# Layer 2 by Strassen's seven products, with statistics on ScalarE and listed orders

## The chip, the cores and the metric

One Trainium2 chip; the kernel runs on one of its cores. The core's engines each work through an instruction queue of their own: TensorE (PE in the profile; PEld are its weight loads), VectorE (DVE), ScalarE (ACT), GpSimd (POOL) and SyncE (SP, which here only issues DMAs). They wait for one another through semaphores. A matmul here multiplies a stationary block of 128 x 128, loaded beforehand, with up to 512 moving columns, and writes into PSUM; the kernel uses 8 PSUM banks of 512 f32 columns on 128 partitions.

The metric is the device time of one execution in microseconds (us). The kernel before takes 298.35 us, the median of three runs (297.99 to 298.51).

## The reference

Two blocks follow each other. The first is a cross attention between 512 tokens and 32 state rows, in 8 batches of 8 heads of 64. The second adds the real part of a two-dimensional Fourier transform to its input, normalises each row and sends it through two dense layers.

```
# block 1, per batch and head: x (512 x 64), state (32 x 64)
a  = softmax(scale * x @ state.T);  xread = a  @ state
a2 = softmax(scale * state @ x.T);  sread = a2 @ x
X  = concat([xread, sread])          # 544 rows; heads side by side: 512 columns
# block 2, per batch: X (544 x 512)
u  = X + real(fft(fft(X, axis=rows), axis=columns))
un = (u - mean(u)) / sqrt(var(u) + 1e-6)          # per row
out = u + relu(un @ w1) @ w2                      # w1 512 x 2048, w2 2048 x 512
```

The output is 8 x 544 x 512 in f32. The matmuls work on bf16.

## The kernel before

The 544 rows of a batch are worked as four row tiles of 128 and 32 left over; the left-over rows of four batches make one tile of 128, the "L" tiles, which come in stages 3 and 7. The kernel runs in stages, one a batch. In stage `b` these stand beside one another: layer 2 of batch `b-1`, layer 1 of batch `b`, the second half of the attention and the Fourier transform of batch `b+1`, the first half of the attention (scores) of batch `b+2`, and loads of x for batch `b+3`.

What the change and the prediction's steps touch, by name and line:

- `layer1(key)`, L908: 16 steps of four 512-column matmuls into `ph` (L920), each followed by a relu on ScalarE into `hT` (L922), which holds the 2048 hidden values of 512 rows, hidden index on the partitions, in bf16. In `hT[:, f, rows]`, `f` counts 16 blocks of 128 hidden values.
- `layer2(key)`, L941: for each row tile `i`, 16 matmuls of 512 columns into one bank `po` (L985), `hT`'s block stationary and `w2`'s rows moving; then `store` (L946) lets VectorE compute `ot = po * rstd + u` (L952) and issues the output DMAs. Rows that come out in reversed order go to `r_dram` first and from there to `out`. The last row tile of the last batch is split into 384 and 128 columns (L977).
- `transform(b)`, L689: the Fourier transform of a batch. `over_s` (`gp`, L774) and `over_d` (`yp`, L670 and L671) are its matmuls. `add` (L675, L682) adds the input rows to give `u`. `centre` (L825) takes the row's mean and variance with VectorE (`bn_stats` L337, `bn_aggr` L339), the reciprocal root on GpSimd (L343, L344), and writes `ub`, the centred rows in bf16, on VectorE (L833) or, for batches 1 and 2, on ScalarE (L831). `turn_u` (L835, the DMA L838) transposes `ub` into `unT` by a DMA. Only batch 0 uses `add_sums`, which takes the row sums in the same pass as the addition (L793), and `centre_sums`, which centres by `-512 u + sum` (L808 to L814) and leaves the factor -1/512 to layer 1's relu.
- `attend(b)`: `scores` (`esp`), `turn_scores` (`eTp`), `xread` (`xfp`, `xrp`, L447; evictions L456), `sread_by_head` (`srp`, L467; L474), and the folds of rows and columns that prepare the Fourier transform (`Sm`, `SS`, `XE`, `XO`, `XQ`, L516 to L536 on VectorE; `XT`, `XEl`, `XOl`, `XQl`, L501 to L513 on GpSimd).

The order is the order in which the Python code calls the engines: written out by hand up to stage 1, and from stage 2 on by `weave`, which sorts the steps of several lists by a position between 0 and 1 that is spread evenly over a range given for each list. All engines keep this order, each for its own instructions; nothing is moved by a scheduler.

PSUM: two banks for `psX`, three for `psQ` and three for `psF` (from which `ph` and `po` come). The pools hand out their buffers in turn. In SBUF the tags `xs`, `xT`, `E`, `ET` and `hT` have two buffers each, `ot` four and `ub` five.

Of the kernel before, what the change touches and what calls it, by code (L numbers as in the profile page):

```python
# [12 lines left out]
F32 = mybir.dt.float32  # L13
BF16 = mybir.dt.bfloat16
I32 = mybir.dt.int32
AF = mybir.ActivationFunctionType
ALU = mybir.AluOpType
PI = math.pi

@with_exitstack  # L30
def kernel(
# [8 lines left out]
    nc = tc.nc  # L40
# [16 lines left out]
    wk = ctx.enter_context(tc.tile_pool(name="wk", bufs=2))  # L57
    opening = ExitStack()
# [628 lines left out]
    flipped = (0, 1, 2)  # L687

    def transform(b):  # L689
# [8 lines left out]
        order = [(0, 1), (1, 0), (0, 0), (1, 1)] if b == B - 1 else [(0, 1), (0, 0), (1, 1), (1, 0)]  # L698
# [135 lines left out]

        def turn_u(k, r, copy=nc.vector.tensor_copy):  # L835
            col = order.index((k, r)) * 128
            if b >= u_by_dma:
                nc.sync.dma_start_transpose(out=unT[:, :, col:col + 128], in_=ub[k, r])  # L838
                return
            tp = qt("tp", BF16)  # L840
            for j in range(DC):
                nc.tensor.transpose(tp[:, 128 * j:128 * j + 128], ub[k, r][:, 128 * j:128 * j + 128], ident)
            copy(unT[:, :, col:col + 128], tp[:, 0:512].rearrange("p (a b) -> p a b", b=128))
# [20 lines left out]
        if b == 2:  # L864
# [7 lines left out]
            lambda: (over_d(0), add(0, 1), add(0, 0)),  # L872
            lambda: centre(0, 1),
            lambda: (centre(0, 0), over_d(1), add(1, 1), add(1, 0)),
            lambda: (turn_u(0, 1), centre(1, 1)),
            lambda: (turn_u(0, 0), centre(1, 0)),
            lambda: turn_u(1, 1),
            lambda: turn_u(1, 0),
# [29 lines left out]
    def layer1(key):  # L908
# [6 lines left out]
        def step(i):  # L915
            ph = psF.tile([128, 512], F32, name="ph", tag="c")
            for f in range(per * i, per * i + per):
                o = (f % per) * n
                for c in range(DC):
# [3 lines left out]
                                 scale=-1.0 / 512 if key == 0 else -1.0 if key in flipped else 1.0)  # L923

        def quarter_step(i, r):
            ph = psF.tile([128, 512], F32, name="ph", tag="c")
            for f in range(4 * i, 4 * i + 4):
                o = 128 * (f % 4)
                for c in range(DC):
# [3 lines left out]
                                 AF.Relu, scale=-1.0 / 512 if key == 0 else -1.0 if key in flipped else 1.0)  # L933
# [5 lines left out]
    later = []  # L939

    def layer2(key):  # L941
# [4 lines left out]
        def store(i, cols):  # L946
# [4 lines left out]
            ot = wk.tile([128, dm], F32, name="ot", tag="ot", bufs=4)  # L951
            nc.vector.scalar_tensor_tensor(ot[:, cols], in0=po_of[i][:, 0:cols.stop - cols.start], scalar=rstd,  # L952
                                           in1=u[:, cols], op0=ALU.mult, op1=ALU.add)
            queue = nc.scalar if key == B - 1 else nc.sync
            if isinstance(dst, bass.AP):
                nc.sync.dma_start(out=dst[:, cols], in_=ot[:, cols])
            elif isinstance(dst, int):
                nc.sync.dma_start(out=l_dram[dst].rearrange("b r n -> (b r) n"), in_=ot)
                for a in range(2):
                    nc.sync.dma_start(out=out[4 * dst:4 * dst + 4, 129 + 272 * a:144 + 272 * a, :].rearrange("b r n -> r b n"),  # L960
                                      in_=l_dram[dst, :, 16 * a:16 * a + 15, :].rearrange("b r n -> r b n"))
                    nc.sync.dma_start(out=out[4 * dst:4 * dst + 4, 272 * a, :].rearrange("b (c n) -> c b n", c=16),
                                      in_=l_dram[dst, :, 16 * a + 15, :].rearrange("b (c n) -> c b n", c=16))
            else:
                b, k, top = dst
                queue.dma_start(out=r_dram[b, k], in_=ot)
                later.append(lambda: queue.dma_start(
                    out=out[b, top:top - 128:-1, :].rearrange("r (c n) -> c r n", c=16),
                    in_=r_dram[b, k].rearrange("r (c n) -> c r n", c=16)))

        def step(i, q):
            if key == B - 1 and i == n - 1:
                cols = slice(0, 384) if q < 2 else slice(384, 512)
                if q % 2 == 0:
                    po_of[i] = psF.tile([128, dm], F32, name="po", tag="c")
                for f in range(8 * (q % 2), 8 * (q % 2) + 8):
                    nc.tensor.matmul(po_of[i][:, 0:cols.stop - cols.start], lhsT=h_of[key][:, f, i * 128:(i + 1) * 128], rhs=w2[:, f, cols],  # L977
                                     start=(f == 0), stop=(f == FC - 1))
                if q % 2:
                    store(i, cols)  # L980
                return
# [9 lines left out]


# [107 lines left out]
    warm(8)  # L1100
    opening.close()
    psX = ctx.enter_context(tc.tile_pool(name="psX", bufs=1, space=bass.MemoryType.PSUM))
    psQ = ctx.enter_context(tc.tile_pool(name="psQ", bufs=3, space=bass.MemoryType.PSUM))
    psF = ctx.enter_context(tc.tile_pool(name="psF", bufs=3, space=bass.MemoryType.PSUM))
# [116 lines left out]
    for b in range(1, B + 1):  # L1221
        reads_next = reads_after
        l2, l2_now = (layer2(b), [l2[7]] + l2[8:]) if b == 1 else (layer2(b) if b < B else [], l2)
# [3 lines left out]
        if b == 1:  # L1227
# [14 lines left out]
            for step in (spreads, M1[2], s2[0], s2[1], L1[0], M1[3], s2[2], s2[3], L1[1], lambda: cast_x(3), turned[3], L1[2],  # L1242
# [7 lines left out]
                step()  # L1250
            continue
# [6 lines left out]
        if b + 2 < B:  # L1258
            scores_next, reads_after = attend(b + 2)
            streams.append(([lambda: (cast_x(b + 2), turned[b + 2]())], 0.2, 0.2))  # L1260
            streams.append((scores_next, 0.5, 1))
        if b + 3 < B:
            streams.append(([lambda: load_x(b + 3)], 0.35, 0.35))
# [3 lines left out]
        weave(*streams)  # L1267

# [29 lines left out]
```

The softmax here doesn't subtract the row's maximum and nothing guards it: scores larger than these inputs give would overflow.

## Time and profile before

| what | us |
|---|---|
| median of three runs | 298.35 |
| span of the profiled execution, first to last instruction | 296.4 |
| 0 to 30: busy PE / DVE / ACT / POOL | 24.9 / 20.9 / 24.0 / 18.9 |
| 30 to 292.8: busy PE / DVE / ACT / POOL | 262.1 / 154.3 / 116.3 / 73.0 |
| 292.8 to 296.4, the last eviction and output write: PE / DVE | 0.2 / 0.35 |
| 139 to 171, one steady stage: busy PE / DVE / ACT / POOL | 32.0 / 19.2 / 13.5 / 7.9 |
| 267 to 293, the last batch's layer 2: busy PE / DVE / ACT / POOL | 26.0 / 4.4 / 4.8 / 0.0 |

The granted TensorE clock was 1.0 in every slice. In the profile a group of instructions stands as line, engine, operation, what it writes and reads, the shape, the count, then its busy time, the mean duration of one in ns, and the idle time of its engine just before, with what ended it. A timeline row has start, duration, engine, line, operation and count; rows of one kind that follow each other are merged. A matmul's duration includes the time in which the next one already runs.

### The profile page before, as it was taken

The page shows a single profiled execution, that of the slowest core. Times are in us where ns is not written, and L with a number is a line of the kernel's source. Part 1 is how long each engine was busy: PE and PEld are TensorE (multiplying, and loading weights), DVE is VectorE, ACT ScalarE, POOL GpSimd, SP SyncE. Part 2 cuts the span into 40 slices and gives each one's busy share as a digit, 9 for nine tenths or more (in the row PEclk, how much of TensorE's full clock was granted, in tenths as well). Part 3 has the DMA queues.
Part 4 walks back from the last instruction along what each step waited for, and adds up shares of the span by engine and source line. Part 5 has one row for each costly group of instructions (what it writes and reads, how often), then busy time and mean ns, then how long its engine had stood idle before and what let it go on. Part 6 is the DMA issues. An engine that isn't in the chain of part 4 may idle for free.

```text
span 296.4 us, 6037 instructions
## 1 busy us (share of the span) xinstructions
PE 287.2 (97%) x2319; PEld 163.4 (55%) x2319; DVE 175.5 (59%) x438; ACT 140.3 (47%) x263; POOL 92.0 (31%) x227
## 2 busy tenths in 40 slices
PE   5999999999999999999999999999999999999995
PEld 4688985545544554566444554455445544555443
DVE  8865789486867659727469394838577664111122
ACT  6887766646815461354523553363525342334200
POOL 6763834293580227102261034302240221000000
PEclk9999999999999999999999999999999999999999
DMA  9999993956965933575344954261433024400345
GB/s 155 194 204 193 155 175 66 174 143 142 178 154 79 242 99 61 121 150 133 82 100 80 187 125 115 54 123 56 125 74 68 20 79 103 105 36 14 94 107 143
DMA packets 110824, 34.86 MB, mean 118 GB/s; under 512 B 101980, under 2 KB 106332, under 8 KB 110796
## 3 DMA queue, kind: packets, MB, share of 16 engines
q1 hardware_dynamic: 100076, 28.72, 45.2%
q0 software_dynamic: 4224, 4.19, 9.1%
q10 hardware_dynamic: 6496, 1.57, 2.6%
q8 instruction: 18, 0.29, 0.5%
q14 instruction: 10, 0.08, 0.1%
HBM read 22.41 MB, written 14.02 MB: 123 GB/s over the span
## 4 chain that ended last, share of the span: by engine, by line
PE 77%; DMA 6%; SPq 5%; POOL 4%; DVE 3%; issue 2%; ACT 2%; POOLq 0%; DVEq 0%
PE po L985 35%; PE ph L920 33%; SPq L145 4%; DMA s_dram<-in_state_dram 3%; PE gp L774 2%; DMA gen<-s_dram 2%; POOL xin L148 1%; SPq L388 1%; PE po L977 1%; PE yp L671 1%; DMA xs<-in_x_dram 1%; PE yp L670 1%; PE xrp L447 1%; PE eTp L434 1%; PE esp L422 1%
## 5 line engine op out<-in xcount | busy, mean ns | idle before, releaser
L985 PE MATMUL po<-w,hT 128*128 128x512 bf16 x496 | 123.4, 379 | 0.0
L922 ACT ACTIVATE hT<-ph 128x512 bf16<-128x512 f32 x112 | 66.8, 597 | 111.6 <-PE ph L920 111.4
L920 PE MATMUL ph<-unT,w 128*128 128x512 bf16 x448 | 113.5, 379 | 0.0
L920 PEld LDWEIGHTS <-w 128*128 128x128 bf16 x576 | 50.4, 98 | 45.8 <-issue 0.6
L985 PEld LDWEIGHTS <-hT 128*128 128x128 bf16 x496 | 46.9, 98 | 47.4
L952 DVE SCALAR_TENSOR_TENSOR ot<-po,rstd,U 128x512 f32<-128x512 f32 (+2 forms) x33 | 24.1, 731 | 49.7 <-PE po L985 44.6
L778 POOL COPY GL<-G 128x128 bf16<-128x128 bf16 x7 | 2.0, 289 | 65.8 <-ACT G L775 65.8
L675 DVE TENSOR_TENSOR U<-yp,XR 128x512 f32<-128x512 f32 x14 | 9.5, 681 | 21.0 <-PE yp L671 21.0
L337 DVE BATCH_NORM_STATS2 st<-U 128x6 f32<-128x512 f32 x32 | 21.8, 681 | 0.1
L344 POOL TENSOR_TENSOR rstd<-rstd,mhalf 128x1 f32<-128x1 f32 x34 | 20.9, 614 | 2.7
L343 POOL TENSOR_TENSOR rstd<-mv,epst 128x1 f32<-128x1 f32 x34 | 6.9, 204 | 45.6 <-DVE mv L339 45.6
L930 PE MATMUL ph<-unT,w 128*128 128x128 bf16 x256 | 15.8, 219 | 0.9 <-DMA w<-in_moe_w_ch_dram 0.6
L930 PEld LDWEIGHTS <-w 128*128 128x128 bf16 x256 | 14.8, 98 | 1.2 <-DMA w<-in_moe_w_ch_dram 0.7
L775 ACT CAST G<-gp 128x288 bf16<-128x288 f32 x28 | 12.8, 482 | 4.9 <-PE gp L774 4.9
L148 POOL CAST xin<-xs 128x2048 bf16<-128x2048 f32 (+1 forms) x9 | 11.7, 1317 | 3.9 <-DMA xs<-in_x_dram 3.8
L932 ACT ACTIVATE hT<-ph 128x512 bf16<-128x512 f32 x16 | 9.4, 598 | 4.4 <-PE ph L930 4.2
L501 POOL COPY XT<-XR 32x514 bf16<-32x514 bf16 x7 | 4.2, 603 | 21.7 <-DVE XR L456 20.7
L833 DVE TENSOR_SCALAR ub<-U,mv 128x512 bf16<-128x512 f32 x20 | 10.2, 511 | 0.8
L455 DVE RECIPROCAL rs<-xrp 128x8 f32<-128x8 f32 x14 | 2.9, 206 | 13.1 <-PE xrp L447 13.1
L456 DVE TENSOR_TENSOR XR<-xrp,rs 128x512 bf16<-128x512 f32 x14 | 9.7, 695 | 0.5
L456 DVE TENSOR_TENSOR XF<-xfp,rs 128x512 bf16<-128x512 f32 x14 | 9.7, 692 | 0.5
L675 DVE TENSOR_TENSOR U<-yp,XF 128x510 f32<-128x510 f32 x14 | 9.4, 673 | 0.0
(240 smaller groups left out, 377.1 us busy)
## 6 DMA issues: line engine op xcount, KB each, us to landing
xs<-in_x_dram SPq DMA_DIRECT2D x22, 256.0 KB, 4.7
w<-in_moe_w_ch_dram POOLq DMA_DIRECT2D x8, 512.0 KB, 9.2
out_dram<-ot SPq DMA_DIRECT2D x15, 256.0 KB, 3.6
r_dram<-ot SPq DMA_DIRECT2D x14, 256.0 KB, 2.2
out_dram<-r_dram SPq DMA_DIRECT2D x14, 256.0 KB, 3.7
xs<-in_x_dram SPq DMA_DIRECT2D x8, 192.0 KB, 4.6
xs<-in_x_dram ACTq DMA_DIRECT2D x2, 256.0 KB
l_dram<-ot SPq DMA_DIRECT2D x2, 256.0 KB
```

Of the source, the lines that this page charges most:

```text
L145: nc.sync.dma_start(out=o, in_=rows)
L148: copy(xin_bufs[b % 2][:, lo:hi, 1:513], xs_of[b].rearrange("p (i c) -> p i c", i=4)[:, lo:hi])
L337: nc.vector.bn_stats(st6, u)
L344: nc.gpsimd.tensor_tensor(rstd, rstd, mhalf, op=ALU.pow)
L456: nc.vector.tensor_tensor(ov, in0=p[ps, :, 0:256].rearrange("p g (h d) -> p g h d", d=D), in1=rs[ps].unsqueeze(3).to_broadcast([n, 2, 4, D ...
L675: nc.vector.tensor_add(u.rearrange("p (k r) -> p k r", r=2), p.rearrange("p (r k) -> p k r", r=2)[:, 0:u.shape[1] // 2, :], x.rearrange("p ...
L775: nc.scalar.copy(G[:, j, :].rearrange("p (i q) -> p q i", q=2), p[:, 0:NM].rearrange("p (q i) -> p q i", q=2))
L920: nc.tensor.matmul(ph[:, o:o + n], lhsT=w1[:, c, f * 128:(f + 1) * 128], rhs=un_of[key][:, c, :], start=(c == 0), stop=(c == DC - 1))
L922: nc.scalar.activation(hT[:, per * i:per * i + per, :].rearrange("p a b -> p (a b)"), ph, AF.Relu, scale=-1.0 / 512 if key == 0 else -1.0 ...
L930: nc.tensor.matmul(ph[:, o:o + 128], lhsT=w1[:, c, f * 128:(f + 1) * 128], rhs=un_of[key][:, c, 128 * r:128 * r + 128], start=(c == 0), st ...
L952: nc.vector.scalar_tensor_tensor(ot[:, cols], in0=po_of[i][:, 0:cols.stop - cols.start], scalar=rstd, in1=u[:, cols], op0=ALU.mult, op1=AL ...
L985: nc.tensor.matmul(po_of[i], lhsT=h_of[key][:, f, i * 128:(i + 1) * 128], rhs=w2[:, f, :], start=(f == 0), stop=(f == FC - 1))
```

## The change

Four things change.

1. Layer 2 of batches 2 to 7 works on two row tiles at a time. With the stationary side cut in two by rows and in two by hidden index (A11, A12, A21, A22, each 128 rows x 1024 hidden values) and `w2` in two by hidden index and in two by columns (B11 to B22, each 1024 x 256), the product is formed by Strassen's seven products in Winograd's form instead of eight. S1, S2, A12-S2 (VectorE) and A21-A11 (GpSimd) are formed per pair, the last two in place in `hT`; T1 to T4 are formed once from `w2`. Each product is 8 matmuls of 256 columns. Partial sums are not kept apart: a product is added in PSUM to what stands in `poA` or `poB`, and after each product VectorE adds the bank, times `rstd`, to `ot`. T1 and T2 lie in one of the two `xs` buffers, T4 in one of `xT`, S1 and S2 in one each of `E` and `ET`, T3 in the part of `stb` of batches 0 to 3.
2. Batches 3 to 7 centre on ScalarE from row sums that come with the addition, and take the variance by a `Square` activation with an accumulator on ScalarE.
3. A `Recorder` stands in for the engines: calls are kept and played in three stretches (up to the end of batch 0's transform; stages 1 and 2; stages 3 to 8), the second and third in listed orders.
4. PSUM banks and `ot` buffers are handed out by lists; from stage 3 on `psQ` has two banks and `psF` four.

```
+ORDERS = {n: [i for p in t.split() for i in range(int(p.split("-")[0]), int(p.split("-")[-1]) + 1)] for n, t in {
...
+    def play(self):
+        order = ORDERS.get(self.stretch) or range(len(self.groups))
+        for n in order:
+            for call in self.groups[n][1]:
+                made = call()
...
-    nc = tc.nc
+    nc = Recorder(tc.nc)
...
-    flipped = (0, 1, 2)
+    flipped, summed = (1, 2), (0,) + tuple(range(3, B))
...
+        def spread_out(k, r):
+            ssq = wk.tile([128, 1], F32, name="ssq", tag="mv", bufs=10)
+            nc.scalar.activation(junk, U[k][:, r, r:r + 512], AF.Square, bias=S_of[k, r][:, 0:1], scale=-512.0, accum_out=ssq)
+            rstd = rstds[k, r] = wk.tile([128, 1], F32, name="rstd", tag="rstd", bufs=16)
+            nc.gpsimd.tensor_scalar(rstd, in0=ssq, scalar1=512.0 ** -3, scalar2=eps, op0=ALU.mult, op1=ALU.add)
+            nc.gpsimd.tensor_tensor(rstd, rstd, mhalf, op=ALU.pow)
+        def centre_out(k, r):
+            t = ub[k, r] = wk.tile([128, 512], BF16, name="ub", tag="ub", bufs=5)
+            ud = U[k][:, r, 0:512] if r == 0 else U[k][:, 1, 512:0:-1]
+            nc.scalar.activation(t, ud, AF.Identity, bias=S_of[k, r][:, 0:1], scale=-512.0)
...
-            lambda: (over_d(0), add(0, 1), add(0, 0)),
-            lambda: centre(0, 1),
-            lambda: (centre(0, 0), over_d(1), add(1, 1), add(1, 0)),
-            lambda: (turn_u(0, 1), centre(1, 1)),
+            lambda: (over_d(0), add_sums(0, 1), add_sums(0, 0)),
+            lambda: centre_out(0, 1),
+            lambda: (centre_out(0, 0), over_d(1), add_sums(1, 1), add_sums(1, 0)),
+            lambda: (turn_u(0, 1), centre_out(1, 1), spread_out(0, 1)),
...
+    def weight_sum(i):
+        T = strassen["T"]
+        o, x, y = ((T[0], B12, B11), (T[1], B22, T[0]), (T[2], B22, B12))[i] if i < 3 else (T[3], B21, T[1])
+        nc.vector.tensor_sub(o, x, y)
...
+            def first_sums():
+                S1, S2 = strassen["S"]
+                nc.vector.tensor_add(S1, A21, A22)
+                nc.vector.tensor_sub(S2, S1, A11)
+            def product(p, lhs, rhs, start, cols=slice(0, 256)):
+                for f in range(8):
+                    nc.tensor.matmul(p[:, cols], lhsT=lhs[:, f, :], rhs=rhs[:, f, cols], start=(start and f == 0), stop=(f == 7), skip_group_check=not start)
...
+            def put(i, c, p, first, cols=slice(0, 256)):
...
+                nc.vector.scalar_tensor_tensor(o[:, at], in0=p[:, cols], scalar=root(), in1=(u if first else o)[:, at], op0=ALU.mult, op1=ALU.add)
...
+                if n == 0:
+                    if r == 0:
+                        first_sums()
+                    a = st["a"] = bank("poA")
+                    product(a, A11, B11, True)
+                    put(0, 0, a, True)
+                elif n == 1:
+                    nc.gpsimd.tensor_sub(A21, A11, A21)
+                    b = bank("poB")
+                    product(b, A12, B21, True)
+                    put(0, 0, b, False)
+                elif n == 2:
+                    product(st["a"], S2, T2, False)
+                    put(0, 1, st["a"], True)
+                    nc.vector.tensor_sub(A12, A12, S2)
+                elif n == 3:
+                    b = st["b"] = bank("poB")
+                    product(b, S1, T1, True)
+                    put(1, 1, b, True)
+                elif n == 4:
+                    product(st["b"], A12, B22, False)
+                    put(0, 1, st["b"], False)
+                    send(0)
+                    if r == 0:
+                        fast[1]()
+                elif n == 5:
+                    product(st["a"], A21, T3, False)
+                    put(1, 1, st["a"], False)
+                elif key == B - 1 and r == 1:
+                    send(1, slice(256, 512))
+                    for lo in (0, 128):
+                        cols = slice(lo, lo + 128)
+                        product(st["a"], A22, T4, False, cols)
+                        put(1, 0, st["a"], True, cols)
+                        send(1, cols)
+                else:
+                    product(st["a"], A22, T4, False)
+                    put(1, 0, st["a"], True)
+                    send(1)
...
+        return p0[:5] + p1[:5] + p0[5:] + p1[5:] if key == B - 1 else p0 + p1
...
-    psQ = ctx.enter_context(tc.tile_pool(name="psQ", bufs=3, space=bass.MemoryType.PSUM))
-    psF = ctx.enter_context(tc.tile_pool(name="psF", bufs=3, space=bass.MemoryType.PSUM))
+    psQ, psF = Banks(tc, middle, "psQ", 3), Banks(tc, middle, "psF", 3)
...
+        if b == 3:
+            nc.play()
+            middle.close()
+            psX = ctx.enter_context(tc.tile_pool(name="psX", bufs=1, space=bass.MemoryType.PSUM))
+            psQ, psF = Banks(tc, ctx, "psq", 2), Banks(tc, ctx, "psf", 4)
...
-        l2, l2_now = (layer2(b), [l2[7]] + l2[8:]) if b == 1 else (layer2(b) if b < B else [], l2)
+        l2, l2_now = (layer2(b), [l2[7]] + l2[8:]) if b == 1 else (None, l2 if b == 2 else layer2_fast(b - 1))
...
+    nc.play()
```

## The prediction

> **What bounds the kernel now.** I read the shares of the span first, then the chain that ended last, then the instructions in order of time, and last the groups by engine. Times are in us.
>
> ```profile
> PE 287.2 (97%) x2319; PEld 163.4 (55%) x2319; DVE 175.5 (59%) x438; ACT 140.3 (47%) x263; POOL 92.0 (31%) x227
> PE   5999999999999999999999999999999999999995
> PE 77%; DMA 6%; SPq 5%; POOL 4%; DVE 3%; issue 2%; ACT 2%; POOLq 0%; DVEq 0%
> PE po L985 35%; PE ph L920 33%; SPq L145 4%; DMA s_dram<-in_state_dram 3%; PE gp L774 2%; DMA gen<-s_dram 2%; POOL xin L148 1%; SPq L388 1%; PE po L977 1%; PE yp L671 1%; DMA xs<-in_x_dram 1%; PE yp L670 1%; PE xrp L447 1%; PE eTp L434 1%; PE esp L422 1%
> ```
>
> TensorE is busy in every slice but the first and the last, and the chain runs through it for 77% of the span. 68% are the two big products: layer 2 (L985) and layer 1 (L920). The other engines wait for it. So a column less on TensorE is time won, as long as nothing makes TensorE wait.
>
> The busy figure of a matmul (379 ns at 512 columns) is no price, since matmuls overlap. The price is the distance from start to start, which the timeline and the chain give:
>
> ```profile
> 19.37 0.27 PE L670 MATMUL yp<-TEO,G 128*128 128x256 bf16 x1 [0.27 <-DVE G L756]
> ...
> 20.24 1.06 PE L404 MATMUL xTp<-ident,xin 128*128 128x128 bf16 x16
> ...
> 22.28 1.95 PE L930 MATMUL ph<-unT,w 128*128 128x128 bf16 x32 [0.29 <-DVE unT L843]
> 24.07 0.39 PE L842 MATMUL tp<-ident,ub 128*128 128x128 bf16 x4
> ```
>
> ```profile
> 278.29 11.22 PE po L985 x52
> 289.51 3.51 PE po L977 x32
> ```
>
> 52 matmuls of 512 columns take 11.22: 0.216 each. Between 19.37 and 20.24 stand eight of 256 columns, each with a new weight load: 0.109 each. 32 of 128 columns, each with its load, take 1.79: 0.056. A weight load (98 ns in its row) thus binds at no width used here.
>
> **TensorE's work.** The change takes out 368 matmuls of 512 columns (six batches of 64, less the last row tile's 16) and the last tile's 32 of L977. It adds 664 of 256 columns and 16 of 128 (12 pairs of row tiles, 7 products of 8, the last product cut in two). Removed: 368 x 0.216 = 79.5, and 3.5, together 83.0. Added: 664 x 0.109 = 72.4, and 16 x 0.056 = 0.9, together 73.3. Net **-9.7**. At 0.110 a piece it is 9.0, at 0.108 it is 10.3.
>
> A rule speaks against this. The Trainium skill (TensorE: Matmul & The Clock Gate, Back-to-back issue gap) gives 131 ns for N=512 and 81 ns for N=128 in a stream of loads and matmuls; an estimate on the line between them is 98 ns for 256, and the change would cost 368 x 0.131 = 48 against 664 x 0.098 = 65, a loss of 17. The rows above, 216 and 56, contradict both ends, and they decide.
>
> **DVE.** The rows that price it:
>
> ```profile
> L952 DVE SCALAR_TENSOR_TENSOR ot<-po,rstd,U 128x512 f32<-128x512 f32 x31 | 23.2, 747 | 47.6 <-PE po L985 44.6 <-DMA unT<-ub 2.6 <-POOL rstd L344 0.3
> L952 DVE SCALAR_TENSOR_TENSOR ot<-po,rstd,U 128x384 f32<-128x384 f32 x1 | 0.6, 616 | 1.9 <-PE po L977 1.9
> L952 DVE SCALAR_TENSOR_TENSOR ot<-po,rstd,U 128x128 f32<-128x128 f32 x1 | 0.4, 351 | 0.3 <-PE po L977 0.3
> L516 DVE TENSOR_TENSOR Sm<-XF,XR 128x1028 bf16<-128x1028 bf16 x7 | 4.9, 696 | 0.3
> L526 DVE TENSOR_TENSOR XE<-SS 128x512 f32<-128x512 f32 x7 | 4.9, 694 | 0.2
> L337 DVE BATCH_NORM_STATS2 st<-U 128x6 f32<-128x512 f32 x32 | 21.8, 681 | 0.1
> 171.00:203.00 32.00, 32.00 (x222) 16.37 (x221) 20.87 (x48) 13.98 (x27) 8.88 (x18) 1.00 0.46 103
> ```
>
> An eviction of 256 columns lies between 351 and 616: 0.48. A batch has 14 of them where it had 4 of 0.747: +3.8. Each pair adds three bf16 sums of 1024 columns on DVE (S1, S2, A12-S2), at Sm's 0.70: +4.2 a batch. Moved to ScalarE (batches 3 to 7): four statistics of 0.681 and 0.182 and four centrings of 0.511, -5.5; the adds that take over the row sums bring accumulator reads (0.082 each) and small adds, +0.8. So a 32 us stage with 20.9 of DVE work becomes one of 30.4 (two pairs less 0.8 each) with 24.2, 80%. ScalarE takes eight passes over 512 columns at 0.724 (its centring row) and four accumulator reads at 0.206: 14.0 + 6.6 = 20.6, 68%. The four T sums (2048 columns, 1.24 each on the line through Sm's 514 and 1028 columns) fall once, in stage 2, 5.0 in all. No engine becomes the bound by its sum; what hides all this is that TensorE has work from layer 1 queued in between.
>
> **What TensorE must now wait for.** Four products of a pair go into poA or poB on top of what has just been evicted, so each must wait for that eviction. The turn costs 0.27 (a 256-column matmul) + 0.05 (yp ends 99.12, its add starts 99.17) + 0.48 + 0.06 (G's copy ends 98.78, yp starts 98.84) = 0.86. I laid the changed TensorE sequence end to end at the distances above and read how much of it lies in each such turn. Nearly all have 0.97 or more; one, before the last product of batch 7, has 0.56: **+0.3**. A relu's turn, 0.38 + 0.05 + 0.60 + 0.06 = 1.09, has 1.1 to 1.3 in its tightest places, and is hidden.
>
> That supposes an idle DVE. In batch 4's first pair it is not: between the eviction of the previous batch's last product (ready at 172.1 of that count) and the one before A12 x B22 stand four evictions, three sums, two 0.69 reads, four small reads of 0.29, two reciprocals of 0.20 and a copy of 0.15: 1.9 + 2.1 + 1.4 + 1.15 + 0.4 + 0.15 = 7.1, so it ends at 179.2, and TensorE wants it at 178.6: 0.6 late. Batch 2's second pair comes out 0.7 late in the same way; batch 5's first pair isn't late. Bounds: 0, and 12 pairs x 0.7 = 8.4. I take 12 x 0.17 = **+2.0**, nearer to the rows I could add up.
>
> **A21-A11 on POOL** has no row. Its two-input rows give 447 ns for 128 columns and 657 for 256, on that line 1.9 for 1024; a cast of 2048 takes 1.89, which bounds it below at 0.95. Its reader, A21 x T3, stands over 5 us later, so alone it costs nothing. But it starts when S1 ends, as DVE goes on to S2:
>
> ```profile
> 65.05 0.60 POOL L343 TENSOR_TENSOR rstd<-mv,epst 128x1 f32<-128x1 f32 x1
> 65.73 1.01 POOL L344 TENSOR_TENSOR rstd<-rstd,mhalf 128x1 f32<-128x1 f32 x1
> 32.46 0.92 DVE L812 TENSOR_SCALAR ub<-U,S 128x512 bf16<-128x512 f32 x1
> ```
>
> Beside DVE sums with two operands in SBUF these two POOL operations took 0.60 and 1.01, where their means are 0.20 and 0.61; DVE's centring took 0.92 beside POOL's fold, and 0.49 the other time (the two average 702 ns). So one holds the other up. That is a lateness of up to 1.9 a pair on DVE; it is in the bounds above and makes a rival.
>
> The Trainium skill (SBUF — State Buffer, Who interferes with whom) says why: a DVE instruction with two SBUF inputs and a POOL instruction that reads SBUF lock each other out, whichever starts first. If every lock reached TensorE, an estimate from its rule and my 1.9 would be 12 x 1.9 = 23, a clear loss.
>
> **Order, banks, buffers, DMAs.** Up to the first second-axis products the four compute engines' order is the same. Behind it, calls and DMA issues are reordered within each engine. There the trace of before has few waits to win: TensorE's gaps after 20 us sum to about 3, of which some 1.3 belong to the head products and stay. I take **-0.7** (0 to -1.5). xs, xT, E and ET keep one buffer each, since T1, T2, T4, S1 and S2 take the other; each is refilled well after its last reader in the listed order (a load of x takes 4.7 and has half a stage): 0, else a wait of a few us for the transposes. The last transpose into batch 7's unT lands (2.4 from issue) some 0.7 before its reader: 0. PSUM goes from 3+3 banks to 2+4, in the turns above.
>
> **The tail.** The last eviction and its 64 KB write are as before (last matmul to end 3.6). A 256 KB write (3.6 to landing) now starts some 0.3 earlier than that one, where before it lay further back: **+0.3**.
>
> **Sum.** 296.4 - 9.7 + 0.3 + 2.0 - 0.7 + 0.3 = 288.6 span. The median of the runs, 298.35, is 1.95 above that span: **290.6**.
>
> **Rivals.**
> 1. DVE falls behind in most pairs, by the lock or the queue: 0.5 more a pair than I took, 12 x 0.5 = 6: 296.6. For it: 80% load in the stage, margins of 0.1 in the turns. Against: S2 has over 1 us to its reader in the pair worked out, most readers more. Chance 0.15.
> 2. Slower: the three sums of a pair read and write hT in eight blocks of 128 columns, a form without a row. If they run at the f32 rate (XE, 694 for 512, so 1.23 for 1024), each costs 0.53 more, 36 x 0.53 = 19; S1, S2 and A12-S2 follow each other through TensorE, and with 60% of it on the path, 11.5, the time is 302. It decides against the change from 0.27 a sum. Against: rows of 256 and 128 bf16 columns differ by 0.06, half the f32 slope, reversed ones too. Chance 0.09.
> 3. The listed order closes all old waits and DVE is never late: 290.6 - 2.0 - 0.8 = 287.8. For it: the turns' margins are positive nearly everywhere. Chance 0.12.
> That the products aren't what the change says is excluded: the program's matmuls count 664 of 256.
> My forecast, 288.5 to 293.5, has 0.64.
>
> **Numbers.** 290.6 is the likeliest case's. Range 287.5 to 297.0: down to rival 3, up to most of rival 1; outside lie rival 2 and the ends, 0.18. A change under 0.2% (0.6) can't be told from none: same 0.02, between rivals 1 and 2. Slower 0.10, faster 0.88.
>
> **What would show it.** 256-column po products at 0.109 from start to start; DVE about 205 us busy, ScalarE about 173; no gap of TensorE over 0.7 in the stages of batches 3 to 7, 2 to 3 us in all; sums at 0.70. Wrong if the sums take over 0.9, if gaps before poA and poB pass 5 in all, or if the 256-column distance passes 0.115.

## The result, and the profile after

The changed kernel takes 313.98 us (median of four runs, 310.61 to 314.19) where the kernel before takes 298.21: 1.051 of it, interval 1.046 to 1.056. It is slower by 15.8, and 290.6 was forecast.

The page of the changed kernel first: the busy shares, the rows of TensorE, of its granted clock and of VectorE in 40 slices (each digit is a share in tenths), and the shares of the chain that ended last.

```profile
PE 281.4 (90%) x2566; PEld 193.6 (62%) x2599; DVE 206.5 (66%) x518; ACT 163.1 (52%) x323; POOL 127.2 (41%) x239
PE   5986982999899999978999999998999999799992
PEclk9997996899999999999999999999999999999997
DVE  8871648548978916799549894797589655342572
PE 63%; DVE 15%; POOL 8%; DMA 5%; issue 5%; ACT 2%; POOLq 0%; DVEq 0%
```

TensorE was full in every slice but the ends; now it has holes, the deepest between 20 and 60 us (a slice is 7.8 us), and in slices there its granted clock falls. VectorE's share of the chain went from 3% to 15%, GpSimd's from 4% to 8%. VectorE is as busy as worked out (206; 205 was forecast), which is partly luck: its instructions took 12.9 more than the medians of their kind (same operation, tiles and shape), where the kernel before has 0.8, and busy time counts instructions that overlap on an engine once. ScalarE is a little less busy (163; 173).

The price of a product held. In the timeline of TensorE, late in the changed kernel (start, duration, engine, line, operation, count; all calls go through the recorder, so every line is L63):

```profile
301.97 1.04 PE L63 MATMUL poB<-w,hT 128*128 128x256 bf16 x8
302.85 1.91 PE L63 MATMUL poA<-stb,hT 128*128 128x256 bf16 x16
304.59 2.22 PE L63 MATMUL poA<-TB,hT 128*128 128x128 bf16 x24
```

24 matmuls of 256 columns take 304.59 - 301.97 = 2.62, 0.109 each. Laid end to end at the distances of before (0.216, 0.109, 0.056, other widths on straight lines between them), TensorE's work is 276.0 us long against 285.7: 9.7 less (33 matmuls of 512 columns are missing in this trace; they are counted in). The span of the profiled execution grew from 296.4 to 312.3 all the same. Taking from each start-to-start distance its own column time, the waits of TensorE come to 30.6 instead of 7.1 (with the 3.1 ahead of its first matmul), and from the last matmul's start to the end of the span there are 5.7 instead of 3.6: -9.7 + 23.5 + 2.1 = 15.9, which is what the span grew by. Of the 23.5, 13.7 lie between 20 and 60 us (14.9 instead of 1.2); the first of Strassen's products starts at 124.8. The other 9.8 lie behind 60 us. From here on, waits summed over a stretch are meant in this way, so time lost to a lower clock counts as a wait.

The waits between 20 and 60 us in TensorE's timeline; the bracket gives the idle time ahead and what ended it:

```profile
25.83 1.89 PE L63 MATMUL ph<-unT,w 128*128 128x128 bf16 x16 [3.38 <-DMA w<-in_moe_w_ch_dram]
...
51.82 0.30 PE L63 MATMUL gp<-TS,XQ 128*128 128x144 bf16 x1 [5.88 <-DVE XQ L63]
...
53.52 0.30 PE L63 MATMUL gp<-TC,XQl 128*128 128x144 bf16 x1 [0.91 <-POOL XQl L63]
```

Followed back, the wait of 5.88 does not come from VectorE's work. VectorE's queue, and then GpSimd's:

```profile
45.72 0.14 DVE L63 CAST XQl<-XEl 32x1 bf16<-32x1 f32 x1 [3.69 <-POOL XEl L63]
```

```profile
25.92 0.20 POOL L63 TENSOR_TENSOR gate<-xs,w 128x4 f32<-128x4 f32 x1 [5.24 <-DMA w<-in_moe_w_ch_dram]
...
39.00 0.29 POOL L63 CAST stb<-gen 32x128 bf16<-32x128 f32 x1 [8.20 <-DMA gen<-s_dram]
39.35 0.21 POOL L63 CAST xin<-xs 128x16 bf16<-128x16 f32 x1
39.49 0.61 POOL L63 COPY XT<-XR 32x514 bf16<-32x514 bf16 x1
...
45.02 0.66 POOL L63 TENSOR_TENSOR XEl<-XT 32x256 f32<-32x256 bf16 x1
```

GpSimd stands 5.24 for the last quarter of `w1` and 8.20 for batch 3's state to come back from `s_dram`. Behind the second wait is queued the copy `XT`, whose input is there at 35.2 (in s4 below it starts then), and behind that `XEl`, for which VectorE waits, and behind that the sums `XQ`, for which TensorE waits. In the kernel before, `XT` stood ahead of the casts that wait for batch 3's state:

```profile
31.03 0.60 POOL L501 COPY XT<-XR 32x514 bf16<-32x514 bf16 x1 [0.96 <-DVE rcs L486]
...
44.59 1.26 POOL L168 CAST stb<-gen 32x128 bf16<-32x128 f32 x4 [0.79 <-DMA gen<-s_dram]
```

A long wait costs more than itself. Windows of the same execution (window, length, then busy time of PE, PEld, DVE, ACT, POOL, the granted clock, the DMA share, GB/s):

```profile
53.00:54.00 1.00, 0.48 (x5) 0.49 (x6) 1.00 (x3) 0.00 (x1) 0.80 (x2) 0.50 1.25 268
55.00:56.00 1.00, 1.00 (x4) 0.44 (x3) 0.00 (x0) 0.40 (x2) 0.00 (x0) 0.50 1.01 151
57.00:58.00 1.00, 1.00 (x19) 0.95 (x17) 0.00 (x0) 0.95 (x3) 0.00 (x0) 1.00 1.21 221
```

After the wait the granted clock is 0.50 until 56.5, and matmuls stand at twice their distances. The two half-clock stretches of the opening add about 1.5 and 1.7 to the waits.

### The profile page after: what moved, and what is told of

Its sections match the earlier page's. It is cut to its first block, busy times and chain, and to the rows that moved or that the text cites. A ratio compares the mean times of both kernels' runs of the same rounds, so it can differ in the third digit from the quotient of the medians.

```text
span 312.3 us, 6711 instructions
## 1 busy us (share of the span) xinstructions
PE 281.4 (90%) x2566; PEld 193.6 (62%) x2599; DVE 206.5 (66%) x518; ACT 163.1 (52%) x323; POOL 127.2 (41%) x239
## 4 chain that ended last, share of the span: by engine, by line
PE 63%; DVE 15%; POOL 8%; DMA 5%; issue 5%; ACT 2%; POOLq 0%; DVEq 0%
PE ph L63 26%; PE poA L63 11%; PE po L63 9%; PE poB L63 8%; DMA w<-in_moe_w_ch_dram 4%; PE gp L63 3%; DVE ot L63 2%; POOL stb L63 2%; PE yp L63 2%; DVE SS L63 2%; DVE Sm L63 2%; DMA unTL<-ub 2%; POOL rstd L63 1%; DVE XR L63 1%; POOL xin L63 1%
## 5 line engine op out<-in xcount | busy, mean ns | idle before, releaser
L63 PE MATMUL ph<-unT,w 128*128 128x512 bf16 (+1 forms) x680 | 123.3, 322 | 4.7 <-DMA w<-in_moe_w_ch_dram 3.4
L63 ACT ACTIVATE hT<-ph 128x512 bf16<-128x512 f32 x128 | 74.0, 596 | 63.1 <-PE ph L63 57.4
L63 PEld LDWEIGHTS <-w 128*128 128x128 bf16 x832 | 65.7, 99 | 44.8 <-DMA w<-in_moe_w_ch_dram 3.7
L63 PEld LDWEIGHTS <-hT 128*128 128x128 bf16 x616 | 58.8, 98 | 25.8 <-DVE hT L63 2.4
L63 POOL TENSOR_TENSOR hT<-hT 128x1024 bf16<-128x1024 bf16 x12 | 26.7, 2228 | 27.2 <-DVE SA L63 27.0
L63 DVE SCALAR_TENSOR_TENSOR ot<-poA,rstd,U 128x256 f32<-128x256 f32 (+1 forms) x37 | 17.4, 471 | 21.1 <-PE poA L63 14.7
L63 PE MATMUL po<-w,hT 128*128 128x512 bf16 x121 | 30.4, 387 | 0.4
L63 ACT CAST G<-gp 128x288 bf16<-128x288 f32 (+2 forms) x31 | 14.0, 476 | 25.4 <-PE gp L63 25.1
L63 PE MATMUL poB<-w,hT 128*128 128x256 bf16 x192 | 24.6, 273 | 2.0 <-DVE hT L63 1.6
L63 POOL COPY XT<-XR 32x514 bf16<-32x514 bf16 x7 | 4.6, 661 | 52.2 <-DVE XR L63 52.2
L63 POOL TENSOR_SCALAR rstd<-ssq 128x1 f32<-128x1 f32 x20 | 4.6, 231 | 45.4 <-ACT junk L63 43.3
L63 POOL TENSOR_TENSOR rstd<-rstd,mhalf 128x1 f32<-128x1 f32 x34 | 22.0, 652 | 0.8
L63 ACT ACTIVATE ub<-U,S 128x512 bf16<-128x512 f32 (+1 forms) x22 | 15.5, 708 | 10.5 <-DVE U L63 7.2
L63 DVE SCALAR_TENSOR_TENSOR ot<-poB,rstd,ot 128x256 f32<-128x256 f32 x24 | 11.4, 479 | 12.5 <-PE poB L63 12.4
L63 POOL CAST xin<-xs 128x2048 bf16<-128x2048 f32 (+3 forms) x14 | 15.2, 1096 | 5.4 <-PE gp L63 5.2
L63 DVE SCALAR_TENSOR_TENSOR U<-yp,XF 128x2 f32<-128x2 f32 (+1 forms) x24 | 10.0, 418 | 10.4 <-PE yp L63 10.2
L63 ACT ACTIVATE junk<-U,S 128x512 bf16<-128x512 f32 x20 | 14.4, 718 | 0.1
L63 PE MATMUL poA<-TB,hT 128*128 128x256 bf16 (+1 forms) x104 | 12.5, 264 | 1.2 <-DVE ot L63 1.0
L63 PEld LDWEIGHTS <-XQ 128*128 128x128 bf16 x56 | 5.7, 103 | 12.4 <-DVE XQ L63 11.5
L63 PE MATMUL gp<-TS,XQ 128*128 128x144 bf16 x28 | 5.7, 240 | 8.5 <-DVE XQ L63 8.5
L63 ACT ACTIVATE E<-esp 128x512 bf16<-128x512 f32 x14 | 8.1, 594 | 9.3 <-PE esp L63 9.3
L63 PE MATMUL poA<-w,hT 128*128 128x256 bf16 x96 | 12.5, 273 | 0.0
```

Source lines behind the costliest of these rows:

```text
L63: self._rec.add(self._name, lambda: f(*args, **kw), key)
```

## The experiments

Theory Q, formed on these rows: the listed order puts calls that wait for a transfer ahead of what TensorE needs, on queues that keep their order. Theory L: GpSimd's sum and VectorE's sums hold each other up. The rivals stand in the expectations. All times are medians; the kernel before had 298.91, 298.2, 297.48, 297.85 and 297.89 beside them in the five groups of runs, so what is compared across groups is the ratio to it, given in brackets; 1% of it is 3.0 us. In edits of a list the numbers are calls, counted in the written order of a stretch.

### Which order costs what

```
+}.items() if n not in (1,)}          # e1: stages 1, 2 in the written order
+}.items() if n not in (1,2)}         # e2: no listed order
+}.items() if n not in (2,)}          # e3: stages 3 to 8 in the written order
+    BANKS.pop(...)                   # the bank lists that belong to them
```

> The changed kernel, with stages 1 and 2 played in the written order and their PSUM banks handed out in turn; stages 3 to 8 keep the listed order. Theory Q (the listed order of stages 1 and 2 puts GpSimd and DMA calls that wait for a transfer ahead of what TensorE needs; 14 us of TensorE's waits between 20 and 60 us come from it): the waits there fall from 14 to about 1.5, time 299 to 302. Rival S (the seven products wait for their own sums and evictions, and the opening only shows it early): time stays at 311 to 315.

305.64 (1.022, interval 1.018 to 1.026; the changed kernel has 1.051). That lies between the theory's range and the rival's. The waits between 20 and 60 us fall from 14.9 to 0.5. The time falls by 2.85% or 8.5 us only, since 5.8 of new waits come between 100 and 140 us, most of them at one sum that is read below.

> The changed kernel with no listed order and no bank lists at all: Strassen and the statistics on ScalarE, in the written order. Theory Q: the opening's 14 us go; in stages 3 to 8 the products' operands were never placed for DVE's queue, so waits there rise by some us against the listed order: 299 to 306. Rival S: 312 or more.

328.37 (1.098): theory Q gave 299 to 306, and the rival's side is right. The written order of stages 3 to 8, with the banks and `ot` buffers in turn, is 7.6% or 22.7 us worse than the listed one with its lists (e1).

> The changed kernel with the listed order kept in stages 1 and 2 and the written order with banks in turn in stages 3 to 8. Theory Q: the opening's loss stays, 312 to 318. Rival O (the listed order as a whole is at fault, late stages too): 305 to 310.

341.45 (1.141): outside both, 27 us worse than the changed kernel (e3 keeps the list of `ot` buffers, and how much of the 27 is due to that is not shown). So the one list wrecks the opening and the other is what makes Strassen's stages bearable; neither had a price in the prediction.

### Taking the opening apart

s1, s4, s5 and s6 edit the list of stages 1 and 2, inside unbroken runs of one engine's calls (s1, s6) or across (s4, s5). Each keeps the edits of the one before it, and all keep the lists of banks.

```
 s1, GpSimd:  -128 132 73 75 126 76 17 124 81 123 21 10 130 74 399 125 8 127 79 129 78 9 80 398 83 77
              +73 75 74 76 10 8 9 79 78 80 77 128 132 126 17 124 81 123 21 130 399 125 127 129 398 83
 s4, TensorE: -59 57 49 43 55 47     +43 57 49 59 55 47       (ScalarE has 44 ahead of 60 already)
 s5, GpSimd:  -19 11 82 84 14 16 12-13 20 18 15     +11 84 14 16 12-13 18 15 19-21 82     (21 from further back, 83 behind 77)
 s6, SP:      -137-138 31 134 143 133 136 30 ...    +31 30 133-136 137-138 143 ...
```

> The changed kernel; in the listed order of stages 1 and 2, eleven GpSimd calls that feed the first-axis products of batch 1 (the copies and sums of the 32 state rows, two clears, one copy) move ahead of the casts that wait for the state's transfer, within one unbroken run of GpSimd calls. Nothing else moves. Theory Q: TensorE's waits of 6.0 and 1.2 at the first-axis products near 46 and 52 us fall below 1.5 together, and the half clock behind them goes: 305 to 309. Rival P (it is the order of the DMA issues on SP, and what GpSimd waits for is late anyway): the two waits stay over 5 in sum, 312 to 315.

311.92 (1.044): the time is all but the rival's, the waits are not. Those at the first-axis products fall below 1, but the next one appears at once: 2.3 at 48 us, again with half a clock behind it.

> Like the run that moves eleven GpSimd calls ahead (311.9), and layer 1's first step of batch 0 stands ahead of its fourth on TensorE and ScalarE; the fourth reads the last quarter of w1, which lands at 25.8. Theory Q: most of the wait of 3.9 at 22 us and the half clock behind it (1.1) go: 307 to 310. Rival (the transfer is needed soon after in any order): 311 to 313.

312.06 (1.049): the rival's value, no change beyond the intervals. The wait of 3.9 at 22 us becomes 1.9 and 3.6 at 24 and 28 us (behind the 3.6 the granted clock stays at 1.00), and at 48 us TensorE stands for a quarter of `w2` that GpSimd issues at 43.8, in TensorE's timeline of this run:

```profile
51.23 1.87 PE L63 MATMUL po<-w,hT 128*128 128x512 bf16 x4 [3.40 <-DMA w<-in_moe_w_ch_dram]
```

> Like the run with eleven GpSimd calls moved ahead and layer 1's first step ahead of its fourth (312.1), and in the first run of GpSimd calls of stage 1 the clears, casts and the mirror stand ahead of the call that waits for the last quarter of w1; three loads of w2 follow that call at once or come behind the first-axis sums. In the run before, TensorE waited 1.9 and 3.6 at 24 and 28 us and 3.6 at 48 us (for a quarter of w2 that GpSimd issued at 43.8). Theory Q: the waits of 28 and 48 us go with their half clocks: 304 to 308. Rival (a chain of transfers behind them sets the time): 310 to 313.

310.73 (1.043): the rival's side. The wait of 28 us falls to 0.8 and the one for `w2` is gone, and one of 4.2 stands in their place, in TensorE's timeline of this run:

```profile
52.59 0.39 PE L63 MATMUL esp<-sT,xT 128*128 128x64 bf16 x8 [4.07 <-DMA sT<-stb]
```

> Like the run with GpSimd's calls of the opening moved (310.7), and in one unbroken run of DMA issues of stages 1 and 2 the six transpositions for batch 2 stand ahead of fourteen loads of x. In the run before, TensorE waited 4.2 at 48 us for such a transposition, with 1.7 of half clock behind it. Theory Q: both go, 304 to 307, which is what the written order of stages 1 and 2 gives (305.6). Rival (the loads are needed next): 309 to 312.

303.33 (1.018, interval 1.015 to 1.022): theory Q, at or a little below what the written order gives (1.022). So the opening's loss is a chain of head-of-line waits (a call that waits for a transfer holds up every call queued behind it), in GpSimd's queue and in SP's; each one taken out shows the next, and only when both queues are in an order that fits the transfers does the time come back. s4 and s5 alone would have spoken for the rival. In the list before s6, six loads of x stand among the six transpositions; the fourteen of the expectation are the loads that then follow them. s6 and e1 end close together, but not for the same reason: s6 keeps 4.1 of waits between 20 and 60 us where e1 has 0.5, and has 2.5 between 100 and 140 us where e1 has 8.0.

### Strassen and the statistics apart

```
 n1: kernel before + centre_out, spread_out, add_sums for batches 3 to 7
 n2: e2, with add, centre (VectorE) in place of add_sums, centre_out, spread_out
 n3: n2, -nc.gpsimd.tensor_sub(A21, A11, A21)  +nc.vector.tensor_sub(A21, A11, A21)
```

> The kernel before with one part of the change: batches 3 to 7 centre and take the variance on ScalarE. No Strassen, no listed order, PSUM as before. Both theories: TensorE's work is the same and VectorE gets lighter: 297 to 300. If ScalarE's longer queue delays the relus of layer 1: 301 to 306.

299.28 (1.0039, interval 1.002 to 1.006): harmless, as expected, and no gain by itself.

> The kernel with Strassen's products as the only part of the change besides two and four PSUM banks from stage 3: statistics and centring on VectorE, written order. Theory: the statistics put 5.5 us a batch back on VectorE, so its queue is later still than in the run with everything in the written order (328.4): 328 to 340. Rival (the statistics on ScalarE were the late ones): below 326.

343.91 (1.149), beyond the theory's 328 to 340 on the far side from the rival: in the written order, the products come later still with the statistics on VectorE.

> The same as the run before it in this list, with A21-A11 on VectorE, ahead of the second product. Theory L: the 9 to 10 us by which A12-S2 is lengthened beside GpSimd's pass go, 8.3 us of sums come: 3 to 10 us shorter than that run. Rival W: 3 or more us longer.

337.41 (1.129): 6.5 shorter, in theory L's range. What the written order does to a product is seen here; first TensorE's row, then VectorE's queue ahead of it:

```profile
170.13 1.03 PE L63 MATMUL poA<-TB,hT 128*128 128x256 bf16 x8 [3.38 <-DVE ot L63]
```

```profile
166.48 0.48 DVE L63 SCALAR_TENSOR_TENSOR ot<-poB,rstd,ot 128x256 f32<-128x256 f32 x1
166.88 0.68 DVE L63 TENSOR_TENSOR SA<-hT 128x1024 bf16<-128x1024 bf16 x1
167.59 0.69 DVE L63 TENSOR_TENSOR SB<-SA,hT 128x1024 bf16<-128x1024 bf16 x1
168.20 0.68 DVE L63 TENSOR_TENSOR XO<-SS 128x510 f32<-128x510 f32 x1
168.92 0.76 DVE L63 TENSOR_TENSOR XQ<-XO 128x256 bf16<-128x256 f32 x2
169.60 0.48 DVE L63 SCALAR_TENSOR_TENSOR ot<-poA,rstd,ot 128x256 f32<-128x256 f32 x1
```

The eviction at 169.60 empties the bank into which the last product adds; the product before it ended on TensorE at 165.0. Two sums for the next pair and the column folds stand ahead of it.

### What the four sums of a pair cost

e1 shows one of them. VectorE and GpSimd in its timelines, and TensorE's row that waited:

```profile
115.00 1.00 DVE L63 TENSOR_TENSOR SA<-hT 128x1024 bf16<-128x1024 bf16 x1
116.04 4.69 DVE L63 TENSOR_TENSOR SB<-SA,hT 128x1024 bf16<-128x1024 bf16 x1
```

```profile
116.22 1.88 POOL L63 CAST xin<-xs 128x2048 bf16<-128x2048 f32 x1
118.07 2.10 POOL L63 TENSOR_TENSOR hT<-hT 128x1024 bf16<-128x1024 bf16 x1
120.13 0.64 POOL L63 CAST XEl<-XT 32x1 f32<-32x1 bf16 x1
```

```profile
120.78 1.50 PE L63 MATMUL poA<-TA,SB 128*128 128x256 bf16 x8 [2.81 <-DVE SB L63]
```

S2 = S1 - A11 takes 0.69 in its median and 4.69 here: it ends, at 120.7, 0.56 behind GpSimd's sum and together with the cast of one column behind that. With GpSimd's sum cut to an eighth (x2 below) the same places read, VectorE first:

```profile
115.97 2.65 DVE L63 TENSOR_TENSOR SB<-SA,hT 128x1024 bf16<-128x1024 bf16 x1
```

```profile
116.15 1.88 POOL L63 CAST xin<-xs 128x2048 bf16<-128x2048 f32 x1
118.00 0.90 POOL L63 TENSOR_TENSOR hT<-hT 128x128 bf16<-128x128 bf16 x1
118.86 0.18 POOL L63 CAST XEl<-XT 32x1 f32<-32x1 bf16 x1
```

Over the whole execution of e1, VectorE's instructions took 12.6 us more than the medians of their kind.

```
 k1: e1, -nc.gpsimd.tensor_sub(A21, A11, A21)   +nc.vector.tensor_sub(...)      (moved in the list, see below)
 x1: e1, all four sums over [:, 0:1] of their eight blocks; S1 and S2 cleared once
 x2: e1, A21-A11 alone over [:, 0:1]      x3: e1, the other three over [:, 0:1]
```

> Like the run with stages 1 and 2 in the written order (305.6), and A21-A11 of every pair formed on VectorE instead of GpSimd, behind A12-S2 or, where its reader comes sooner, just ahead of it. Theory L (GpSimd's pass and VectorE's two-operand sums hold each other up; one S2 took 4.69 instead of 0.69 us beside GpSimd): VectorE gets 12 x 0.69 = 8.3 more work and loses some 9 of 12.5 us of lengthened instructions; the wait of 3.0 at 118 us and the half clock behind it go: 299 to 303. Rival W (VectorE's queue is the limit by its amount of work): 305 to 310.

307.97 (1.031, 2.7 us worse than e1): rival W's side. VectorE's lengthening fell from 12.6 to 3.9, and one of the moved sums came 4.9 late behind the column folds, with a half clock of 2.2. From TensorE's timeline of this run:

```profile
163.87 1.89 PE L63 MATMUL poA<-stb,hT 128*128 128x256 bf16 x8 [4.78 <-DVE hT L63]
```

> Like the run with stages 1 and 2 in the written order (305.6), but S1, S2, A12-S2 and A21-A11 are formed over one of their eight blocks of 128 columns only; the rest of S1 and S2 stays zero and the rest of A12 and A21 stays as it was, so the products are not those of the reference. All instructions stay, their waits too. Theory D (the sums' time on VectorE and GpSimd, with their mutual holding up, makes the products late): the waits of 100 to 240 us fall from about 11 to below 4: 296 to 300. Rival T (the turns of the banks and the place of the calls make them late, whatever the sums take): 302 to 306.

295.15 (0.992, interval 0.989 to 0.994): theory D's side, a little below its range. Against e1 that is 3.0% or 9.0 us, so much do the four sums cost there. The waits between 100 and 240 us fall from 9.7 to 0.2.

> Like the run with stages 1 and 2 in the written order (305.6), with A21-A11 alone formed over one block of eight (the products are not the reference's). GpSimd loses some 22 us of work and VectorE keeps its own. Theory L (GpSimd holds VectorE up): most of the 10.5 us that all four sums cost together comes from here: 296 to 300. Theory D (VectorE's own time for its three sums): 302 to 305.

297.02 (0.997, interval 0.995 to 0.999): in theory L's range. GpSimd's sum alone is worth 7.5 of the 9.0; 2.9 of waits are left between 100 and 240 us. VectorE's lengthening falls to 4.5. About half of the 7.5 comes from the one place shown above: the wait for S2 falls from 2.8 to 0.8, and the half clock behind it (3.41 us long in e1) doesn't come: 2.0 and about 1.7.

> Like the run with stages 1 and 2 in the written order (305.6), with S1, S2 and A12-S2 formed over one block of eight and A21-A11 whole on GpSimd (the products are not the reference's). VectorE loses some 17 us of work. Theory L: 301 to 305. Theory D: 295 to 299.

298.93 (1.003): within theory D's range. VectorE's three sums are worth 5.8, with 4.3 of waits left there. Against x1, VectorE's three sums alone cost 1.6 (x2) and GpSimd's alone 3.3 (x3), both together 9.0. That they hold each other up is one reason that the rows show; that a small lateness is hidden and a large one is not may be another, and these runs don't divide the two. In x3 VectorE's instructions still took 11.2 more than their medians, so its lengthening alone does not set the time. Nor does k1 speak for the lock alone: there 8.7 of lengthening went and 8.2 of sums came, and the time rose.

### The ends, and a version with less of it

```
 t1: e1, end of the list  -833 827 836 829 839   +827 833 829 836 839     (TensorE; VectorE and SP likewise)
                          717 (transposition of the second L tile) ahead of six output writes on SP
 tk: t1 with A21-A11 on VectorE, behind the second product's eviction
 q1: kernel before, layer2_fast for batches 6 and 7, all sums on VectorE      q2: for batch 6 alone
```

> Like the run with stages 1 and 2 in the written order (305.6), with two places of the late order changed: the last products end with the row tile that is split, so that the 256 KB write of the other row tile is issued earlier, and the transposition of the second L tile's rows is issued ahead of six output writes. Theory: last matmul to end falls from 6.1 to about 4, the wait of 1.7 for the L tile goes: 302 to 304. Rival (both are hidden by something else): 305 to 306.

302.83 (1.018, interval 1.012 to 1.023): in the theory's range, though the interval overlaps e1's. From the last matmul's end to the end of the span 4.8 instead of 6.1, and the L tile's wait is gone.

> Like the run with the two places of the late order changed, and A21-A11 on VectorE, behind the eviction of the second product (in the earlier run with this sum on VectorE one of them came 4.9 us late and a half clock of 2.2 followed). Theory L: 299 to 302. Rival W (VectorE's amount of work): 303 to 307.

302.15 (1.014): not told from t1, so neither theory. In its first pair A21 is overwritten before S1 reads it, so that pair's S1 is another sum; the instructions are the same.

> The kernel before, written order, with Strassen's products in batches 6 and 7 only, where VectorE is busy 12 to 30% in the profile of before: all four sums on VectorE, poA in the two banks that the attention leaves free, A21-A11 of batch 7 formed while layer 1 still runs. TensorE's columns fall by a third of 9.7, 3.2. Theory (the sums cost nothing where VectorE is idle): 294.5 to 297. Rival (the last stage, all products and no layer 1, is limited by VectorE at 10.8 of 12.2 us): 297.5 to 301.

302.78 (1.016): beyond the rival. In batch 7 S1 is formed from an A21 that already holds A11-A21. The stage of batch 6 ran with waits of 0.6 and 0.4; the last stage had 3.6 of waits for VectorE, and the tail from the last matmul's end grew from 3.4 to 7.2, as the reversed rows are finished last and go through `r_dram`.

> The kernel before, written order, with Strassen's products in batch 6 alone, where layer 1 of batch 7 stands between the products and VectorE is 12 to 46% busy. All four sums on VectorE. TensorE's columns fall by a sixth of 9.7, 1.6; the same stage in the run with batches 6 and 7 had 0.6 and 0.4 of waits. Theory (the products pay where VectorE is idle): 296.3 to 297.6 beside 297.9 for the kernel before. Rival (the added sums of the weights in batch 6's layer 1 stage cost more than 1): 298 to 299.5.

297.48 beside 297.89 (0.999, interval 0.997 to 1.001): inside the theory's range, and not told from no change. Its profiled execution spans 295.3 us, which executions of the kernel before reach too (295.3 to 298.5). No version that keeps the reference's result was found that is surely faster than the kernel before.

## Why the prediction was wrong, step by step

The sum forecast a span of 288.6; 312.3 came. Its terms:

- TensorE's work, -9.7: -9.7, since the distance at 256 columns is 0.109. The sums on VectorE take 0.68 to 0.69 in their medians, evictions 0.478 (0.48 was taken). The rival "sums at the f32 rate" is out. The rows decided rightly against the rule of the Trainium skill (TensorE: Matmul & The Clock Gate, Back-to-back issue gap): its 131 and 81 ns were not seen here, where the distances are 216 and 56. A loss came, but from another cause than the one worked out from it.
- The last product's turn, +0.3: 0.29.
- **Order, banks, buffers, DMAs: "I take -0.7 (0 to -1.5)": +13.7 in the opening alone.** This is the step that failed. It said that behind the opening "calls and DMA issues are reordered within each engine", and asked only which old waits that could close, not which new ones it opens. The list could be read: on GpSimd the call that waits for the last quarter of `w1` and casts of state that come by way of `s_dram` were ahead of the first-axis sums, on TensorE layer 1's fourth step was ahead of its first, on SP six loads of x stood among the six transpositions for batch 2. Each of these names a transfer whose landing stands in the trace of before (the last quarter of `w1`: 12.6 us from issue, at 26.4). At most 1.5 of gain was possible, and nearly 14 of loss was; a range from 0 down had no reason that excluded a loss. s6 shows the cause: with the order of the two queues changed and nothing else but one TensorE step, the ratio is 1.018 instead of 1.051, 9.6 of 15 us.
- VectorE's lateness, +2.0: about 10 behind 60 us, with the first axis, the L tile and ScalarE's part in it. The mechanism was named (the lock beside A21-A11, and a queue at 80% load), and 8.4 stood as its bound, but the value was taken from two places that could be added up by hand. x2 says what GpSimd's sum is worth in e1's order: 7.5. The sum on GpSimd took 2.23, where 1.9 was taken. The sign that was named for it, gaps before `poA` and `poB` of over 5 in all, did not show (3.1 in the changed kernel): most of the waits came ahead of other matmuls.
- The tail, +0.3: +2.1. Four writes are issued one after the other on SP from 306.1 to 309.2, with a wait of 1.4 for a write of reversed rows among them, while the last eviction ends at 307.2; in the kernel before, the last write was issued as its eviction ended. "Some 0.3 earlier" was a count of matmuls, not of DMA issues. t1 shows that the order matters: the same writes in another order end 1.3 sooner after the last matmul than in e1.
- Of the rivals, the first (the lock or the queue, 6 on top of the 2.0) was right in kind, 8 where about 10 came; alone it would have ended at 296.6, still faster. The slower one named the wrong mechanism, and its limit of 0.27 a sum is 9.7 / 36, which leaves out the other terms and its own 60%; with them it is 7.75 / (36 x 0.6) = 0.36. None asked what the new order could make wait behind the first second-axis products (19.4 us), up to which the order is the same.

What stays open: how the opening's loss divides between GpSimd's and SP's queue, since the waits replace one another, and which of the 9.8 us of waits behind 60 us belong to the order of stages 3 to 8 and which to the sums, beyond the 9.0 that x1 took out of e1.

## What to carry to other kernels

When calls are reordered, walk each in-order queue, GpSimd's and SP's first, and put beside every call that waits for a transfer what is queued behind it and when the transfer lands; a change of order has no sign until that is done. Work that is moved to a half-idle engine must be priced together with what is moved beside it: the two halves of Strassen's sums cost 1.6 and 3.3 us alone and 9.0 together. A bound on a queue's lateness should be taken from its worst burst, not from the places that are easy to add up.

## What the runs showed of the hardware

- **The clock.** Behind the first 10 us, and but for the last stretch, which runs into the end, every stretch at a granted clock of 0.50 lasted 3.41 us or twice that in these traces. They came with waits of TensorE of 1.8 to 5.9 us and reached up to 6.0 us past its restart, where matmuls stood at twice their distances. The length of the wait doesn't decide it alone: waits of 1.8 (e3) and 2.2 (s1) were followed by a half clock, and waits of 2.3 and 3.5 (n2), 2.7 (tk), 3.4 (n3, e3) and 3.5 (s4) by full speed. In the changed kernel waits up to 1.7 kept 1.00. The Trainium skill (TensorE: Matmul & The Clock Gate, What's actually happening) gives an idle window of about 3.4 us to the half clock and as much to the full one; the length of the stretches agrees, and the way in came after shorter waits too.
- **The lock.** The Trainium skill (SBUF — State Buffer, Who interferes with whom) says that the order of issue decides which of the two blocks the other. Here a VectorE sum was held off for two GpSimd instructions in a row, a cast and a sum (4.69 instead of 0.69), and did not get between them; the cast of one column behind them then took 0.64, where it took 0.18 in x2. With the GpSimd sum cut to an eighth (x2) the same VectorE sum took 2.65, and the short GpSimd sum 0.90 where its median is 0.43: there it was GpSimd's sum that came second.
